# Order of the second expert's loads, of the first dense splits, and the PSUM banks of the dense first layer

## The chip, the core and the metric

One core of one Trainium2 chip runs the whole program. The metric is the device time of one execution in microseconds (us). PE is TensorE, ACT ScalarE, DVE VectorE, POOL GpSimd; SP is the engine whose queue issues nearly all DMAs here.

## What is computed

Three stages follow one another: a gated linear attention, a mixture of eight experts with one expert per token, and a dense layer pair with an ELU between.

```python
# attention, B=4, H=8, S=768, D=48: state over time
state = alpha[t] * state + outer(k[t], v[t]);  y[t] = q[t] @ state
# experts: x [3072, 384], 8 experts, F = 1024
idx = argmax((xn @ en.T) / tau);  gate = softmax(...)[idx]
out[mask] = gate * (relu(x[mask] @ w1[e]) @ w2[e])
# dense: w_in [384, 2048], w_out [2048, 384]
h = x @ w_in;  g = where(h > 0, h, exp(min(h, 0)) - 1);  result = g @ w_out
```

## The kernel before

Every factor of the expert and dense products is split into a high and a low part, and three matmuls (high x high, high x low, low x high) stand for one. ACT makes the high part by a copy with rounding, DVE the low part by a subtraction.

**Attention** (`fast`, `ending`) computes the tokens and scatters each tile of 128 of them with an indirect DMA on POOL (`put`, L583) into the DRAM tensor `xs`, sorted by expert. `load_rows` reads one expert's rows back into the tile `xr`, of which there is one.

**Experts** (`moe1`). A block is (e, f), expert and 128 of its 1024 hidden columns, 64 blocks. `mm1(e, f)` makes `h` in a bank of the pool `psG` (three banks, tag `g`) with 9 matmuls (L996 to L998); ACT makes `hh` (L1000) and DVE `hl` (L1001). `mm2(e, f)`, one block later, adds 9 matmuls to the three banks `y` of the pool `psA` (L1028 to L1030). In blocks f = 4, 5, 6 `turn(e + 1, f - 4)` transposes the next expert's rows from `xr` (L977) and splits them (`evict`, L1018, L1019); after the last of these the next `load_x` goes out. Behind the last block of an expert `y[0]` and `y[2]` are copied by ACT and `y[1]` by DVE (L1038 to L1042) into `x2T`, at a column offset that is known only at run time (`off_i`). Experts are taken in the order of their size; `CAPS` gives the columns each one has, from 432 down to 368. Expert e's columns stand in `x2T` behind those of e - 1.

In the same loop, counted by n, `split_piece` splits the weights of the next expert (L200, L203) and orders the next weight load from SP (L171). `load_d` loads pieces of the dense weights as 64-bit numbers (L224), and `decode` turns them into 32-bit ones: one `Square` on ACT (L242), three operations on DVE (L238 to L240), two on POOL (L243, L244). `split_dense` (L258, L259) splits the decoded weights by blocks of the dense stage: four of `wi` in the last iterations n = 61 to 64, two of `wo`. The iteration n = 64 holds only the last `mm2`.

Between the first two blocks and the rest stands an If (L1055): its usual branch is empty, its Else (`fix`) repairs rare cases and reads and rewrites `xr` and `xs`. Behind the join each engine brings the counts of its semaphores in line (L1055 in the trace).

**Dense** (`moe2`). u counts six groups of 512 columns, m sixteen blocks of 128 of the 2048 hidden columns. `mm1(u, m)` makes `h` from `xh`, `xl` with 9 matmuls (L1184) in a bank of the pool `psH2` (four banks); then follow DVE `mn` = min(h, 0) (L1186), ACT `Exp` (L1187), DVE `g` (L1190), which reads the bank last, ACT `gh` (L1193) and DVE `gl` (L1194), which `flush` issues only in the next block, behind that block's `mn`. `mm2`, three blocks later, makes 12 matmuls into four banks of `psO` (L1205 to L1207). In u = 0 each block also carries two `split_dense`. `load_u(u + 1)` at m = 8 splits the next 512 columns by `split_x` (L1103, L1104). For u = 0 these splits stand in the last `mm2` of the experts, between the copies of `y`.

The order of the instructions of each `manual_schedule` block is written out by hand; instructions of different blocks and the If are put together by the scheduler.

Of the kernel before, what the change touches and what calls it, by code (L numbers as in the profile page):

```python
# [8 lines left out]
F32 = mybir.dt.float32  # L9
F32R = mybir.dt.float32r  # L10
# [9 lines left out]
E, F, F2 = 8, 1024, 2048  # L20
# [10 lines left out]
KD = DM // 128  # L31
# [24 lines left out]
U = 512  # L56
# [6 lines left out]
def fused_kernel(ctx, tc, qk, a, v, emb, w12, wi, wo, cst, sel, cols, out):  # L63
    nc = tc.nc
    PS = bass.MemoryType.PSUM
# [4 lines left out]
    stage = ctx.enter_context(tc.tile_pool(name="stage", bufs=2 * PIECES))  # L70
# [81 lines left out]
    raw, whi, wlo = {}, {}, {}  # L152
# [67 lines left out]
    def load_d(j, pool):  # L220
        if j < len(dq):
            nm, s, src = dq[j]
            t = pool.tile([128, HS], I64, bufs=2, name="raw64")
            nc.sync.dma_start(out=t, in_=src[:, s * HS:(s + 1) * HS])  # L224
            dbuf[j] = t
# [726 lines left out]
    def moe1(x2T, xr0, t0, fix, es):  # L952
        with ExitStack() as st:
            xT_p = st.enter_context(tc.tile_pool(name="xT", bufs=2, side="right"))
            h_p = st.enter_context(tc.tile_pool(name="h", bufs=2, side="right"))
            xr, xT, hb, acc = {0: xr0}, {}, {}, {}
            first, freed = [], []

            def load_x(e):
                if e < E:  # L960
                    xr[e] = xr_p.tile([128, 4, DM], F32, name="xr")
                    load_rows(xr[e], e, [0, DM], puts[-2:-1] if e == 1 else [])

            def turn(e, kk):
                if e >= E:
                    return
                if kk == 0:
                    xT[e] = (xT_p.tile([128, KD, CAP], F32R, tag="xh", name="xh"),
                             xT_p.tile([128, KD, CAP], F32R, tag="xl", name="xl"))
                t = psT.tile([128, CAPR], F32, name="t") if e else t0[kk]  # L970
                blocks = 4 if CAPS[e] > 384 else 3
                for r in range(blocks):
                    pr = min(128, CAPR - r * 128)
                    w = min(128, CAP - r * 128)
                    rows = xr[e][:pr, r, kk * 128:(kk + 1) * 128]
                    if e:
                        nc.tensor.transpose(t[:, r * 128:r * 128 + pr], rows, c["ident"][:pr, :pr])  # L977
                    else:
                        nc.tensor.matmul(t[:, r * 128:r * 128 + w], rows, c["ident"][:pr, :w], start=False, stop=(r == 3))
                evict(e, kk, t)  # L980
                if kk == KD - 1:
                    xr.pop(e)
                    if e:
                        load_x(e + 1)
# [36 lines left out]
            def mm2(e, f):  # L1021
                if f == 0:
                    acc[e] = [psA.tile([128, CAP], F32, name=f"y{d}")[:, :CAPS[e]] for d in range(KD)]
                n = CAPS[e]
                hh, hl = (h[:, :n] for h in hb.pop((e, f)))
                for d in range(KD):
                    wh, wl = wblk(e, f * FW + DM + d * 128, 128)
                    nc.tensor.matmul(acc[e][d], wh, hh, start=(f == 0), stop=False)  # L1028
                    nc.tensor.matmul(acc[e][d], wh, hl, start=False, stop=False)  # L1029
                    nc.tensor.matmul(acc[e][d], wl, hh, start=False, stop=(f == FB - 1))  # L1030
                if f == FB - 1:
                    o1 = nc.scalar.value_load(off_i[0:1, e:e + 1], min_val=0, max_val=N)
                    o2 = nc.vector.value_load(off_i[0:1, e:e + 1], min_val=0, max_val=N)
                    y = acc.pop(e)
                    if e == E - 1:
                        for nm in ("xh2", "xl2"):
                            first.append([stage.tile([128, U], F32R, tag="raw", name=nm) for _ in range(KD)])
                    nc.scalar.activation(out=x2T[:, 0, bass.ds(o1, n)], in_=y[0], func=AF.Copy)  # L1038
                    nc.vector.tensor_copy(x2T[:, 1, bass.ds(o2, n)], y[1])
                    if first:  # L1040
                        split_x(x2T, *first, 0, 0)
                    nc.scalar.activation(out=x2T[:, 2, bass.ds(o1, n)], in_=y[2], func=AF.Copy)  # L1042
                    if first:
                        split_x(x2T, *first, 0, 1)
                        split_x(x2T, *first, 0, 2)

            EARLY = 2
            with tc.manual_schedule():
# [17 lines left out]
            psT = st.enter_context(tc.tile_pool(name="psT", bufs=2, space=PS))  # L1066
            dc = st.enter_context(tc.tile_pool(name="dc", bufs=2))
            with tc.manual_schedule():
                load_d(0, dc)
                load_d(1, dc)  # L1070
                load_x(1)
                LAG = 1
                blocks = [(e, f) for e in range(E) for f in range(FB)]
                for n in range(EARLY, len(blocks) + LAG):
                    if n < len(blocks):
                        e, f = blocks[n]
                        mm1(e, f)
                        if n == EARLY:
                            mm2(*blocks[n - LAG - 1])
                        if f >= 4 and f < 4 + KD:  # L1080
                            turn(e + 1, f - 4)
                    if n >= LAG:
                        mm2(*blocks[n - LAG])
                    if n > 2:
                        split_piece()
                        if n % 2:
                            split_piece()
                    if freed:
                        load_d(freed.pop(), dc)
                    j = (n - 2) * 4 // 7  # L1090
                    if j >= 0 and j != (n - 3) * 4 // 7:
                        decode(j, dc, dense)
                        freed.append(j + 2)
                    if n > len(blocks) - 4:
                        split_dense("wi", n - len(blocks) + 3, dense)
                        if n > len(blocks) - 2:
                            split_dense("wo", n - len(blocks) + 1, dense)
            return first, dense

    def split_x(x2T, xh, xl, u, kk):  # L1100

        src = x2T[:, kk, u * U:(u + 1) * U]
        nc.scalar.activation(out=xh[kk], in_=src, func=AF.Copy)  # L1103
        nc.vector.tensor_tensor(xl[kk], src, xh[kk].bitcast(F32), op=ALU.subtract)  # L1104
# [43 lines left out]
    def moe2(x2T, first, dense):  # L1148
        with ExitStack() as st:
# [2 lines left out]
            g_p = st.enter_context(tc.tile_pool(name="g2", bufs=5))  # L1152
            o_p = st.enter_context(tc.tile_pool(name="o2", bufs=5))
            psO = st.enter_context(tc.tile_pool(name="psO", bufs=4, space=PS))
            psH = st.enter_context(tc.tile_pool(name="psH2", bufs=4, space=PS))
            x2, gb, acc, stores = {0: first}, {}, {}, []
            low = []

# [14 lines left out]
                x2[u] = (xh, xl)  # L1173

            def mm1(u, f):
                ps = psH.tile([128, U], F32, name="h2")
                xh, xl = x2[u]
                wh, wl = dblk("wi", f)
                w = [(wh[:, kk * 128:(kk + 1) * 128], wl[:, kk * 128:(kk + 1) * 128]) for kk in range(KD)]
                terms = [t for kk in range(KD) for t in ((w[kk][0], xh[kk]), (w[kk][1], xh[kk]), (w[kk][0], xl[kk]))]  # L1180
                if u == f == 0:
                    terms = [terms[n] for n in (0, 1, 3, 4, 6, 7, 2, 5, 8)]
                for n, (l, x) in enumerate(terms):
                    nc.tensor.matmul(ps, l, x, start=(n == 0), stop=(n == len(terms) - 1))  # L1184
                mn = e_p.tile([128, U], F32, name="mn")
                nc.vector.tensor_scalar(mn, ps, 0.0, None, op0=ALU.min)  # L1186
                nc.scalar.activation(out=mn, in_=mn, func=AF.Exp)  # L1187
                flush()
                g = e_p.tile([128, U], F32, name="g")
                nc.vector.scalar_tensor_tensor(g, mn, -1.0, ps, op0=ALU.add, op1=ALU.max)  # L1190
                gh = g_p.tile([128, U], F32R, tag="gh", name="gh")
                gl = g_p.tile([128, U], F32R, tag="gl", name="gl")
                nc.scalar.activation(out=gh, in_=g, func=AF.Copy)  # L1193
                low.append(lambda: nc.vector.tensor_tensor(gl, g, gh.bitcast(F32), op=ALU.subtract))  # L1194
                gb[u, f] = (gh, gl)
# [34 lines left out]
            blocks = [(u, m) for u in range(NU) for m in range(M)]  # L1230
# [18 lines left out]

    shared = ExitStack()  # L1250
    psG = shared.enter_context(tc.tile_pool(name="psG", bufs=3, space=PS))
    xr_p = shared.enter_context(tc.tile_pool(name="xr", bufs=1, side="right"))
    x0 = attention()
    with tc.tile_pool(name="x2T", bufs=1) as p, ExitStack() as es:
        x2T = p.tile([128, KD, N + CAP], F32, name="x2T")
        first, dense = moe1(x2T, *x0, es)
        shared.close()
        with tc.manual_schedule():
            moe2(x2T, first, dense)


_OUTS = [((N, DM), "float32")]
# [74 lines left out]
```

## Time and profile before

| | us |
|---|---|
| median of the runs shown (794.42, 795.0, 795.1) | 795.0 |
| the profiled execution, its own time | 796.37 |
| its span, first to last instruction | 794.6 |

| engine | busy us | share of the span |
|---|---|---|
| PE | 768.8 | 97% |
| DVE | 521.5 | 66% |
| ACT | 363.1 | 46% |
| POOL | 188.8 | 24% |

The attention stage ends near 156 us, the experts run to 386 us, the dense stage to the end. The granted TensorE clock is 1.00 in each stretch from 100 us on. In the stretch 200 to 350 us PE is busy for the whole time. The page is read as follows: "busy" is time in instructions, a release in square brackets names what ended the idle time just before an instruction, and a line "x3" merges neighbours of one kind. Matmuls overlap, so their spacing, and not their length, is what one costs.

### The profile page before, as it was taken

To read this page: it belongs to the slowest core of one execution; us is meant where nothing else is said; L and a number is where in the kernel's file an instruction comes from. 1 tells how busy PE (TensorE), PEld (TensorE's weight loads), DVE (VectorE), ACT (ScalarE), POOL (GpSimd) and SP (SyncE) were. 2 spreads that over 40 slices of the span, in tenths; PEclk is the share of its full clock that TensorE was granted. 3 is DMA by queue.
4 is the path that set the end of the run, shared out by engine and by line. 5 is a ranking of instruction groups with operands and counts; after the bars stand their busy time and mean duration, and the time that the engine had idled before them with its cause. 6 is when DMAs were issued, how large, how long until landed. Compare 5 with 4: busy or idle time off the path is not lost.

```text
span 794.6 us, 13699 instructions
## 1 busy us (share of the span) xinstructions
PE 768.8 (97%) x5077; PEld 699.0 (88%) x5077; DVE 521.5 (66%) x1001; ACT 363.1 (46%) x802; POOL 188.8 (24%) x217
## 2 busy tenths in 40 slices
PE   7999998889999999999999999999999999999996
PEld 4888887579999999999898899999999999999996
DVE  6789899946877877896576755454555545545442
ACT  4668787435455455553545433233333323323331
POOL 5544667313433433342000020020002002002002
PEclk9899999999999999999999999999999999999999
DMA  9999873357565666661000010010001001000001
GB/s 240 263 269 246 247 187 96 124 170 195 180 198 186 202 204 202 208 200 44 1 1 1 1 40 1 0 40 1 1 1 40 1 1 40 1 0 33 9 1 40
DMA packets 44804, 77.82 MB, mean 98 GB/s; under 512 B 11958, under 2 KB 18230, under 8 KB 44734
## 3 DMA queue, kind: packets, MB, share of 16 engines
q1 hardware_dynamic: 41662, 67.47, 30.2%
q0 software_dynamic: 3072, 9.45, 3.2%
q8 instruction: 40, 0.66, 0.4%
q14 instruction: 30, 0.25, 0.1%
HBM read 64.69 MB, written 12.22 MB: 97 GB/s over the span
## 4 chain that ended last, share of the span: by engine, by line
PE 38%; issue 30%; DVE 3%; POOL 3%; ACT 2%; DMA 1%; POOLq 0%; SPq 0%; ACTq 0%
PE h L1184 6%; PE y L1028 5%; PE y L1030 4%; PE y L1029 4%; PE h L998 4%; PE h L996 4%; PE h L997 4%; POOL out_dram L1218 2%; PE o L1207 2%; PE o L1205 2%; PE o L1206 2%; PE t L977 1%; DVE dlo L259 1%; DVE g L1190 1%; DVE mn L1186 1%
## 5 line engine op out<-in xcount | busy, mean ns | idle before, releaser
L1186 DVE TENSOR_SCALAR mn<-h 128x512 f32<-128x512 f32 x96 | 66.3, 690 | 139.6 <-PE h L1184 139.6
L1187 ACT ACTIVATE mn<-mn 128x512 f32<-128x512 f32 x96 | 60.7, 632 | 171.7 <-DVE mn L1186 171.7
L1207 PE MATMUL o<-dwo,gl 128*128 128x384 f32 x384 | 129.4, 337 | 1.4 <-DVE gl L1194 1.4
L1206 PE MATMUL o<-dlo,gh 128*128 128x384 f32 x384 | 128.4, 334 | 0.0
L1205 PE MATMUL o<-dwo,gh 128*128 128x384 f32 x384 | 128.2, 334 | 0.0
L1184 PE MATMUL h<-xh,dwi 128*128 128x512 f32 x288 | 112.7, 391 | 0.6 <-ACT x2T L1042 0.6
L1184 PE MATMUL h<-xh,dlo 128*128 128x512 f32 x288 | 113.2, 393 | 0.0
L1184 PE MATMUL h<-xl,dwi 128*128 128x512 f32 x288 | 112.5, 392 | 0.0
L1218 POOL DMA_INDIRECT out_dram<-ob,ids x24 | 23.7, 987 | 340.3 <-ACT ob L1215 336.7
L1193 ACT ACTIVATE gh<-g 128x512 fp32r<-128x512 f32 x96 | 60.7, 633 | 77.9 <-DVE g L1190 77.9
L1000 ACT ACTIVATE hh<-h 128x432 fp32r<-128x432 f32 (+6 forms) x64 | 32.4, 507 | 105.1 <-PE h L998 100.5
L203 DVE TENSOR_TENSOR wlo<-raw,whi 128x512 fp32r<-128x512 f32 x96 | 72.8, 786 | 5.6 <-ACT whi L200 5.6
L1190 DVE SCALAR_TENSOR_TENSOR g<-mn,h 128x512 f32<-128x512 f32 x96 | 66.1, 689 | 15.2 <-ACT mn L1187 14.8
L1205 PEld LDWEIGHTS o<-dwo,gh 128*128 128x128 f32 x384 | 72.0, 187 | 4.2
L1206 PEld LDWEIGHTS o<-dlo,gh 128*128 128x128 f32 x384 | 72.0, 187 | 4.0
L1207 PEld LDWEIGHTS o<-dwo,gl 128*128 128x128 f32 x384 | 72.2, 188 | 2.1 <-DVE gl L1194 1.7
L1028 PE MATMUL y<-hh,whi 128*128 128x432 f32 (+6 forms) x192 | 68.3, 356 | 0.0
L243 POOL TENSOR_SCALAR dg<-dg 128x384 f32<-128x384 f32 x32 | 42.1, 1316 | 107.4 <-ACT dg L242 107.3
L996 PE MATMUL h<-xh,whi 128*128 128x432 f32 (+6 forms) x192 | 66.5, 347 | 0.7 <-ACTq L1055 0.7
L1001 DVE SCALAR_TENSOR_TENSOR hl<-h,hh 128x432 fp32r<-128x432 f32 (+6 forms) x64 | 36.7, 573 | 46.4 <-ACT hh L1000 45.0
L1194 DVE TENSOR_TENSOR gl<-g,gh 128x512 fp32r<-128x512 f32 x96 | 65.7, 684 | 1.2 <-ACT gh L1193 1.1
L998 PE MATMUL h<-xh,wlo 128*128 128x432 f32 (+6 forms) x192 | 66.4, 346 | 0.0
(216 smaller groups left out, 1506.2 us busy)
## 6 DMA issues: line engine op xcount, KB each, us to landing
raw<-in_w_dram SPq DMA_DIRECT2D x96, 256.0 KB, 3.1
qk<-in_qk_dram SPq DMA_DIRECT2D x40, 192.0 KB, 5.0
vt<-in_v_dram SPq DMA_DIRECT2D x24, 256.0 KB, 6.0
raw<-in_wi_dram SPq DMA_DIRECT2D x16, 384.0 KB, 3.8
raw<-in_wo_dram SPq DMA_DIRECT2D x16, 384.0 KB, 3.8
xr<-xs SPq DMA_DIRECT2D x7, 576.0 KB, 5.4
at<-in_alpha_dram SPq DMA_DIRECT2D x40, 99.0 KB, 5.6
xs<-zero SPq DMA_DIRECT2D x7, 288.8 KB, 6.2
```

The source lines that it names most:

```text
L203: nc.vector.tensor_tensor(l[:, sl], r, h[:, sl].bitcast(F32), op=ALU.subtract)
L996: nc.tensor.matmul(ps, wh, xh[:, kk], start=(kk == 0), stop=False)
L998: nc.tensor.matmul(ps, wl, xh[:, kk], start=False, stop=(kk == KD - 1))
L1028: nc.tensor.matmul(acc[e][d], wh, hh, start=(f == 0), stop=False)
L1184: nc.tensor.matmul(ps, l, x, start=(n == 0), stop=(n == len(terms) - 1))
L1186: nc.vector.tensor_scalar(mn, ps, 0.0, None, op0=ALU.min)
L1187: nc.scalar.activation(out=mn, in_=mn, func=AF.Exp)
L1190: nc.vector.scalar_tensor_tensor(g, mn, -1.0, ps, op0=ALU.add, op1=ALU.max)
L1194: low.append(lambda: nc.vector.tensor_tensor(gl, g, gh.bitcast(F32), op=ALU.subtract))
L1205: nc.tensor.matmul(o_, gh[:, sl], wh, start=(f == 0), stop=False)
L1206: nc.tensor.matmul(o_, gh[:, sl], wl, start=False, stop=False)
L1207: nc.tensor.matmul(o_, gl[:, sl], wh, start=False, stop=(f == M - 1))
```

## The change

Four edits. `load_x(1)` is written ahead of the two first `load_d`. The splits of the first 512 dense columns leave the copies of `y` and are written ahead of the last `mm2` of the experts, in iteration n = 64. The dense first layer takes its banks from `psG`, three of them, in place of a pool of four of its own, and its first block uses the usual order of terms. The decodes start at n = 5 and not 2, and end at n = 60 and not 57.

```diff
                     y = acc.pop(e)
-                    if e == E - 1:
-                        for nm in ("xh2", "xl2"):
-                            first.append([stage.tile([128, U], F32R, tag="raw", name=nm) for _ in range(KD)])
                     nc.scalar.activation(out=x2T[:, 0, bass.ds(o1, n)], in_=y[0], func=AF.Copy)
                     nc.vector.tensor_copy(x2T[:, 1, bass.ds(o2, n)], y[1])
-                    if first:
-                        split_x(x2T, *first, 0, 0)
                     nc.scalar.activation(out=x2T[:, 2, bass.ds(o1, n)], in_=y[2], func=AF.Copy)
-                    if first:
-                        split_x(x2T, *first, 0, 1)
-                        split_x(x2T, *first, 0, 2)
...
+                load_x(1)
                 load_d(0, dc)
                 load_d(1, dc)
-                load_x(1)
...
+                    if n == len(blocks):
+                        for nm in ("xh2", "xl2"):
+                            first.append([stage.tile([128, U], F32R, tag="raw", name=nm) for _ in range(KD)])
+                        for kk in range(KD):
+                            split_x(x2T, *first, 0, kk)
                     if n >= LAG:
                         mm2(*blocks[n - LAG])
...
-                    j = (n - 2) * 4 // 7
-                    if j >= 0 and j != (n - 3) * 4 // 7:
+                    j = (n - 5) * 4 // 7
+                    if j >= 0 and j != (n - 6) * 4 // 7:
                         decode(j, dc, dense)
...
-            psH = st.enter_context(tc.tile_pool(name="psH2", bufs=4, space=PS))
...
-                ps = psH.tile([128, U], F32, name="h2")
+                ps = psG.tile([128, U], F32, tag="g", name="h2")
...
-                if u == f == 0:
-                    terms = [terms[n] for n in (0, 1, 3, 4, 6, 7, 2, 5, 8)]
...
-    xr_p = shared.enter_context(tc.tile_pool(name="xr", bufs=1, side="right"))
+    rest = ExitStack()
+    xr_p = rest.enter_context(tc.tile_pool(name="xr", bufs=1, side="right"))
...
-        shared.close()
+        rest.close()
         with tc.manual_schedule():
             moe2(x2T, first, dense)
+        shared.close()
```

## Rows read from the trace of the kernel before

**Rows 1.** Waits of PE: who waited for whom, us in total, times, longest.

```profile
PE o L1207 <- DVE gl L1194: 1.4, 1, 1.4
...
PE t L977 <- DMA xr<-xs: 1.2, 1, 1.2
...
PE h L1184 <- ACT x2T L1042: 0.6, 1, 0.6
```

**Rows 2.** Timeline of SP's queue: start us, length us, instruction.

```profile
166.68 0.82 SPq L224 DMA_DIRECT2D raw<-in_wi_dram  x2
172.58 1.23 SPq L274 DMA_DIRECT2D xr<-xs  x2
...
196.87 4.72 SPq L171 DMA_DIRECT2D raw<-in_w_dram  x3
201.63 0.43 SPq L224 DMA_DIRECT2D raw<-in_wi_dram  x1
```

**Rows 3.** Instructions of line 1055, the If: count, ns each, first and last start.

```profile
L1055 SPq EVENT_SEMAPHORE  x9: 17/17/17, 168.1 to 171.4; - x9
...
L1055 SPq COMPARE_BRANCH  x1: 73/73/73, 167.5 to 167.5; - x1
```

**Rows 4.** Timeline of PE across the transposes of expert 1, two blocks.

```profile
175.18 0.36 PE L998 MATMUL h<-xh,wlo 128*128 128x432 f32 x1
...
177.40 0.46 PE L1028 MATMUL y<-hh,whi 128*128 128x432 f32 x1
...
180.84 0.36 PE L998 MATMUL h<-xh,wlo 128*128 128x432 f32 x1
...
181.66 0.46 PE L1028 MATMUL y<-hh,whi 128*128 128x432 f32 x1
```

**Rows 5.** Timeline of PE from the experts into the dense stage.

```profile
386.12 0.33 PE L1029 MATMUL y<-hl,whi 128*128 128x368 f32 x1
386.29 0.33 PE L1030 MATMUL y<-hh,wlo 128*128 128x368 f32 x1
...
389.59 0.39 PE L1184 MATMUL h<-xh,dwi 128*128 128x512 f32 x1
...
395.83 0.33 PE L1205 MATMUL o<-dwo,gh 128*128 128x384 f32 x1
```

**Rows 6.** Timeline of ACT in the same stretch.

```profile
384.41 0.52 ACT L258 ACTIVATE dwo<-wd 128x384 fp32r<-128x384 f32 x1
...
386.70 0.46 ACT L1042 ACTIVATE x2T<-y 128x368 f32 x1
387.06 1.14 ACT L1103 ACTIVATE xh<-x2T 128x512 fp32r<-128x512 f32 x2
388.10 0.52 ACT L258 ACTIVATE dwi<-wd 128x384 fp32r<-128x384 f32 x1
388.51 0.52 ACT L258 ACTIVATE dwo<-wd 128x384 fp32r<-128x384 f32 x1
```

**Rows 7.** Timeline of DVE in the same stretch.

```profile
385.09 0.55 DVE L259 TENSOR_TENSOR dlo<-wd,dwo 128x384 fp32r<-128x384 f32 x1
...
387.71 1.30 DVE L1104 TENSOR_TENSOR xl<-x2T,xh 128x512 fp32r<-128x512 f32 x2 [0.19 <-ACT xh L1103]
...
389.39 0.55 DVE L259 TENSOR_TENSOR dlo<-wd,dwo 128x384 fp32r<-128x384 f32 x1
389.86 0.68 DVE L1186 TENSOR_SCALAR mn<-h 128x512 f32<-128x512 f32 x1
```

**Rows 8.** Timeline of DVE and PE around the tenth and the thirteenth dense block.

```profile
430.99 0.69 DVE L1190 SCALAR_TENSOR_TENSOR g<-mn,h 128x512 f32<-128x512 f32 x1 [0.16 <-ACT mn L1187]
...
432.73 0.39 PE L1184 MATMUL h<-xh,dwi 128*128 128x512 f32 x1
```

**Rows 9.** Timeline of DVE and PE in expert 1's third block.

```profile
202.67 0.60 DVE L1001 SCALAR_TENSOR_TENSOR hl<-h,hh 128x432 fp32r<-128x432 f32 x1
...
203.91 0.35 PE L1029 MATMUL y<-hl,whi 128*128 128x432 f32 x1
```

## The prediction

> **What bounds the kernel now.** I read three views, in this order. First the waits of PE: behind the branch PE waits for another engine or a DMA only three times, 1.2 us for the second expert's rows, 0.6 us at the start of the dense stage, 1.4 us for one `gl` [rows 1]. So from 177 us on the end of the kernel is PE's own work plus those three waits, and what an edit is worth is what it takes off them. Then PE's timeline around each wait, for its full price, which is more than the idle time since the pipeline fills again. Last the timelines of ACT, DVE and SP's queue, for what ended each wait and what comes late next.
>
> The 1.4 us wait decides how the dense part of the change is to be counted. In the first 512 columns (u = 0) ACT and DVE also split the dense weights, and they work as one chain, each step waiting for the other: `mn`, `Exp`, `g`, `gh`, two `split_dense`, next `mn`. It hangs on the first `mn` at 389.86 [rows 7] and not on PE, which is several us ahead of it. Its period is a little longer than PE's, and at the ninth block, with `load_u(1)` added to it, PE catches up with it and waits 1.4 us for `gl` [rows 1]. The next blocks each start as their `gl` arrives. So time that PE gains before 389 us is given back there, except for what the chain gains too.
>
> **Part 1, the second expert's rows first.** SP's queue now issues the two 64-bit loads at 166.68, then the branch, and behind the branch stand nine semaphore waits from 168.1 to 171.4; only then does `load_x(1)` go out, at 172.58 [rows 2, 3]. The nine waits bring the counts of SP's DMA semaphores in line after the If, so they wait for the two 64-bit loads to land. The loads, later in the program than the branch, were drawn ahead of it by the scheduler. `load_x(1)` can't be: the Else path reads and writes that tile. Inside one hand-ordered block the queue keeps the written order even where a later load would be ready: the 64-bit load at 201.63 goes out behind the three weight loads that began at 196.87 and were waiting for DVE [rows 2]. So with `load_x(1)` at the head of the block, the 64-bit loads must follow it behind the branch, and the nine waits no longer contain them. `load_x(1)` still waits for the last scatters into `xs`, as the 64-bit loads do before 166.68. I put its issue 1.2 us after that (172.58 less 171.4, the cost of the register load and address), at about 167.9. From issue to PE's first transpose it took 4.0 us (172.58 to 176.6, which is 177.40 less the 0.8 us of a turn without a wait, below), so it would come at about 171.9. PE is ready for it at 175.4, after the last matmul of that block at 175.18 [rows 4]. If the 64-bit loads were served ahead of it, with the 4.7 us that they now take (166.68 to 171.4), it would come no earlier than now: that is the lower bound.
>
> What the wait costs: from the last first-layer matmul to the first `y` matmul across a transpose, 175.18 to 177.40 is 2.22 us; the next block without a wait takes 180.84 to 181.66, 0.82 us [rows 4]. Gain **1.40 us**, bounds 0 (that case, or the queue's order doesn't change) and 1.40. Nothing after it gives it back: until 386 us PE has no other wait [rows 1], and DVE follows PE there.
>
> The 64-bit loads come about 2 us later, and the decodes are moved by three blocks, so nothing waits for them. Of the moved step every instruction counts: 4 per decode on DVE and ACT, two on POOL, and on SP the load of the piece after next. DVE had room at the end (it does nothing but `hl` in blocks 59 and 60), and the last decode comes a block before the first `split_dense`, which reads other pieces. The new positions (n - 5 in place of n - 2, both in steps of 4 per 7 blocks) meet every phase of the 8 blocks of an expert once in 56 blocks, as the old ones do; only the expert differs. The tightest place now is expert 1's third block, where `hl` ends at 203.27 and PE takes it at 203.91: 0.64 us [rows 9]. That phase now falls on expert 4. Blocks are shorter there: a `y` matmul of 368 columns is spaced 0.17 us [rows 5], so 36 columns less on 18 matmuls make 0.30 us a block, 0.6 us over the two blocks in which DVE falls behind. The 0.64 us are used up. Cost 0 to 0.3 us, I take **0.05 us**.
>
> **Part 2, the dense start.** Now PE ends `y` with the matmul at 386.29, waits until ACT's copy of `y[2]`, issued from L1042, frees the bank, and reaches block (0, 1) at 389.59 [rows 1, 5]. Without a wait the first dense matmul would start at 386.46, and with 27 matmuls from 389.59 to 395.83 (0.231 each) block (0, 1) at 388.54: PE alone would gain 1.05 us. The `psG` banks are free by then (last read by expert 7's `hl`, ahead of the `dlo` at 385.09 [rows 7]), and the splits are made ahead of `y`. But by the chain, the gain is the shift of the first `mn`. I lay out the new order with the spacings of the rows [rows 6, 7]. ACT: `dwo` at 384.41, 0.41 later the three `xh`, 0.52 apart (1.14 less 0.62 for two), the third ending at 386.49; then `y[0]`. DVE: `dlo` at 385.09, `xl` at 385.56, 386.17 and 386.78 (spacing 0.61), the third ending at 387.47. All stand before PE's terms ask for them: the third, sixth and ninth matmul of 386.46, that is 386.92, 387.62 and 388.31, so the usual order of terms costs nothing (0.6 us to spare). Here is the new wait: the copy of `y[2]` writes at an offset known only at run time into the columns that `xl` reads, so it waits for the third `xl`: 387.50 to 387.96. Behind it on ACT stand `dwi` (387.86) and `dwo` (388.27 to 388.79); on DVE their `dlo` at 388.40 and 388.87, and 0.47 later `mn`, at **389.34** in place of 389.86. PE's block ends before (388.70), so it isn't PE that holds it.
>
> Gain **0.52 us**. Bounds: 1.05 if the copies of `y` don't wait for the splits (then all of PE's gain is kept), and 0 if register loads on ACT or DVE stand in the way. I take the value laid out; it comes from the nearest rows.
>
> **Three banks for four.** `h` of block n + 3 needs the bank of block n, free when `g` of n is done. The tightest row: `g` of block (0, 9) ends at 431.68 and block (0, 12) starts at 432.73, 1.05 us later, with four banks [rows 8]. `gl` of a block is issued behind `mn` of the next one, so close to a whole period of the chain after its `g`, while PE asks for it only 2.4 us after that bank (nine matmuls of 0.231 and two of 0.17); so `gl` stays the wait that ends last. Cost **0**, bounds 0 and 0.5 (my 0.52 us of lost distance still leave 0.5). The Trainium skill speaks against this part: Perfetto Trace Analysis, Optimization Strategy, says that a gap that repeats on the engine that should be saturated can mean too few buffers for the next tile. By it the first blocks of u = 0 would show a gap each; by the row they would not, and the sum stays.
>
> **The sum.** 1.40 + 0.52 - 0.05 = 1.87 us. The profiled execution took 796.37 us (span 794.6), so it would take 794.5. The median of the runs shown is 795.0, 1.4 us below that execution; the same 1.87 us off it give **793.1 us**, 0.24% faster. Less than about 0.2% (1.6 us, so anything above 793.4) can't be told from no change.
>
> **Rivals.** (a) The 64-bit loads are still drawn ahead of the branch, so `load_x(1)` goes out as late as now. For: the scheduler did it once. Against: the kept order at 201.63. Only 0.5 us are left: 794.5. (b) The dense start gives nothing, because the chain starts no earlier: 1.40 - 0.05, 793.6. For: the same instructions stand between the last `hl` and `mn`, in another order only. Against: the layout above. (c) All of PE's 1.05 us is kept, because the copies don't wait: 792.6. (d) Slower: DVE falls behind in the expert stage. Place: the block with the copies of `y`, a split and a decode, and the next with two splits and a decode, now in shorter blocks. It decides once `hl` comes after PE wants it, so when the 0.64 us are gone, and the price is each excess. If all 8 rounds of decodes had 0.6 us too much, 4.8 us: 797.9. Against: only one round has this phase, so one excess and not eight.
>
> **How the numbers follow.** Forecast (both parts as laid out) 0.62; (a) 0.12; (b) 0.09; (c) 0.12; (d) 0.05. The forecast is within about 0.4 us of 793.1, as the runs shown spread by 0.7 us; about three quarters of it lies below 793.4. Faster by over 0.2%: 0.48 from it, 0.12 from (c), 0.03 from (b), 0.63 together. Slower 0.05. The rest, 0.32, is within. The range takes in (c) and most of (a): 792.3 to 794.5.
>
> **What would show it.** Part 1: SP issues the rows of expert 1 near 168 us and the 64-bit loads behind them; PE's wait on `xr` at L977 is gone; PE is 1.4 us earlier at 200 us. Part 2: the first dense matmul follows the last `y` matmul by 0.17 us, `mn` comes about 0.5 us earlier against it, and PE's wait for `gl` grows from 1.4 to about 1.9 us. No wait of PE on `g`. Wrong: `load_x(1)` at 172 us; a wait on `hl`; or the wait for `gl` no longer than now (then all of 1.05 us is kept).

## The result, and the profile after

The changed kernel takes 807.35 us (median of 4 runs, 806.47 to 808.43); the kernel before, run beside it, 794.71 (794.33 to 795.1). The ratio is 1.0147, 95% interval 1.0122 to 1.0173: about 12 us slower, where 1.9 us faster was forecast. The profiled execution took 807.04 us, with a span of 805.3. Line numbers shift with the change: the `o` matmul of L1207 stands at L1201 here, the `idl` transfers of L1225 at L1219.

First the waits of PE in the changed kernel (who waited for whom, us in total, times, longest):

```profile
PE y L1028 <- ACT hh L1000: 8.9, 1, 8.9
...
PE o L1201 <- DVE gl L1188: 1.6, 1, 1.6
...
PE y L1029 <- DVE hl L1001: 0.5, 1, 0.5
```

Against [rows 1], the wait of 1.2 us for `xr` is gone, as forecast, and so is the 0.6 us at the dense start. The wait for `gl` is 1.6 us in place of 1.4. New is a single wait of 8.9 us for `hh`, in the expert stage's last blocks. PE's timeline shows it, and what follows it:

```profile
379.43 0.33 PE L998 MATMUL h<-xh,wlo 128*128 128x368 f32 x1
388.68 0.67 PE L1028 MATMUL y<-hh,whi 128*128 128x368 f32 x1 [8.92 <-ACT hh L1000]
389.88 0.68 PE L1029 MATMUL y<-hl,whi 128*128 128x368 f32 x1 [0.53 <-DVE hl L1001]
390.36 0.51 PE L1030 MATMUL y<-hh,wlo 128*128 128x368 f32 x1
390.66 0.51 PE L1028 MATMUL y<-hh,whi 128*128 128x368 f32 x1
...
397.11 0.33 PE L1030 MATMUL y<-hh,wlo 128*128 128x368 f32 x1
397.28 0.39 PE L1178 MATMUL h<-xh,dwi 128*128 128x512 f32 x1
```

The matmuls behind the wait come 0.30 us apart (390.36 to 390.66), where the same matmul is spaced 0.17 us in [rows 5]. The table by stretches gives the clock that goes with it (us; busy of PE, PEld, DVE, ACT, POOL; granted clock, share of the DMA engines, GB/s):

```profile
350.00:378.00 28.00, 28.00 (x168) 27.93 (x168) 19.99 (x34) 11.99 (x25) 9.55 (x9) 1.00 0.29 82
378.00:389.00 11.00, 2.08 (x12) 1.74 (x10) 1.28 (x3) 1.29 (x4) 0.65 (x1) 0.72 0.53 36
389.00:393.00 4.00, 3.47 (x11) 3.12 (x11) 3.04 (x5) 0.82 (x3) 1.63 (x2) 0.50 0.00 0
393.00:397.00 4.00, 4.00 (x26) 4.00 (x25) 2.03 (x5) 2.54 (x6) 0.00 (x0) 1.00 0.05 0
```

PE stood idle for 8.9 us; the granted clock is 0.50, the 1.2 GHz level, while it starts again, and 1.00 behind 393 us. So the stall costs 11.6 us: 9.1 from 379.60, when the first `y` matmul was due, to 388.68; 0.5 for `hl`; 2.0 for matmuls at the lower clock (from 388.68 to 393.09 pass 4.4 us, where eleven spacings of 0.17 make 1.9; the 2.5 between are these 0.5 and 2.0). All other changes together are worth less than 2 us.

Who holds `hh`? ACT's timeline:

```profile
373.74 0.48 ACT L1000 ACTIVATE hh<-h 128x368 fp32r<-128x368 f32 x1 [2.56 <-PE h L998]
387.71 0.55 ACT L242 ACTIVATE dg<-raw 128x384 f32<-128x384 f32 x1 [13.50 <-DMA raw<-in_wo_dram]
388.16 0.46 ACT L1000 ACTIVATE hh<-h 128x368 fp32r<-128x368 f32 x1
```

ACT stood for 13.5 us at the `Square` of the last decode, in iteration n = 60, because the last 64-bit load had not landed; `hh` of the block that PE had finished was queued behind it. And the load was late because of SP's queue:

```profile
358.19 1.76 SPq L224 DMA_DIRECT2D raw<-in_wo_dram  x2
360.24 15.73 SPq L1219 DMA_DIRECT2D idl<-xs  x3
377.20 0.35 SPq L224 DMA_DIRECT2D raw<-in_wo_dram  x1
```

Between the last but one and the last 64-bit load stand three `idl` transfers, which belong to the dense stage: at its head (L1217 to L1219) it copies the token numbers of each expert's rows from `xs` to `idl`, eight transfers of up to 432 numbers, which nobody needs before the first stores. They write one tensor, so each waits until the one before has landed, and SP waits with it. The load's buffer was free at 366.6 us, behind the last read of decode 29 on DVE:

```profile
366.06 0.56 DVE L240 SCALAR_TENSOR_TENSOR wd<-raw,wd 128x384 int32<-128x384 int32 x1
```

It went out at 377.2 and landed at 387.6 by the trace's DMA events. In the kernel before, the same stretch of SP's queue reads:

```profile
359.13 0.37 SPq L224 DMA_DIRECT2D raw<-in_wo_dram  x1
359.79 52.42 SPq L1225 DMA_DIRECT2D idl<-xs  x7
```

There the last 64-bit load is ahead of all seven; the eighth, which is the first in order, went out at 174.7 us.

At the front of the stage the change did what it should. SP now issues the rows of expert 1 first, in place of [rows 2]:

```profile
167.09 1.22 SPq L274 DMA_DIRECT2D xr<-xs  x2
168.43 0.97 SPq L224 DMA_DIRECT2D raw<-in_wi_dram  x2
```

### The profile page after: what moved, and what is told of

It is laid out like the page before. It is cut to its first block, busy times and chain, and to the rows that moved or that the text cites. A ratio compares the mean times of both kernels' runs of the same rounds, so it can differ in the third digit from the quotient of the medians.

```text
span 805.3 us, 13698 instructions
## 1 busy us (share of the span) xinstructions
PE 769.9 (96%) x5077; PEld 698.9 (87%) x5077; DVE 524.1 (65%) x1001; ACT 362.3 (45%) x802; POOL 188.0 (23%) x217
## 4 chain that ended last, share of the span: by engine, by line
PE 36%; issue 30%; DVE 5%; DMA 3%; POOL 2%; ACT 2%; SPq 0%; POOLq 0%; ACTq 0%
PE h L1178 6%; PE y L1028 4%; PE y L1029 4%; PE y L1030 4%; PE h L997 4%; PE h L998 4%; PE h L996 4%; POOL out_dram L1212 2%; PE o L1201 2%; PE o L1199 2%; PE o L1200 2%; DMA idl<-xs 2%; DVE dlo L259 1%; DMA raw<-in_wo_dram 1%; PE t L977 1%
## 5 line engine op out<-in xcount | busy, mean ns | idle before, releaser
L1201 PE MATMUL o<-dwo,gl 128*128 128x384 f32 x384 | 129.9, 338 | 1.6 <-DVE gl L1188 1.6
L203 DVE TENSOR_TENSOR wlo<-raw,whi 128x512 fp32r<-128x512 f32 x96 | 75.4, 812 | 5.3 <-ACT whi L200 4.5
L1201 PEld LDWEIGHTS o<-dwo,gl 128*128 128x128 f32 x384 | 72.1, 188 | 3.2 <-DVE gl L1188 2.6
L243 POOL TENSOR_SCALAR dg<-dg 128x384 f32<-128x384 f32 x32 | 41.8, 1305 | 127.8 <-ACT dg L242 127.6
L1029 PE MATMUL y<-hl,whi 128*128 128x432 f32 (+6 forms) x192 | 67.0, 349 | 0.5 <-DVE hl L1001 0.5
L1030 PE MATMUL y<-hh,wlo 128*128 128x432 f32 (+6 forms) x192 | 66.9, 348 | 0.0
```

The costliest lines, as they stand in the source:

```text
L203: nc.vector.tensor_tensor(l[:, sl], r, h[:, sl].bitcast(F32), op=ALU.subtract)
L1201: nc.tensor.matmul(o_, gl[:, sl], wh, start=False, stop=(f == M - 1))
```

## The experiments

**How they are read.** The attention stage, which no kernel here changes, ended at other times in each execution: the first `h` matmul of the experts came between 157.5 us and 164.8 us in the 14 profiled ones. That alone spreads the times by several us, and a difference of 1 or 2 us stays inside the intervals of most comparisons. Behind that point, and behind the wait on `xr`, kernels with the same instructions repeat within about 0.05 us, with two exceptions: 0.27 us that ACT loses at one dense block of some kernels (last paragraph), and 0.25 us in e11 at block 53, where a 64-bit load landed 6.3 us after its issue (5.1 in e1) and its decode waited. So beside the measured ratio, each experiment is read by three stretches of its PE timeline, as differences from the kernel before (us, minus is faster). The stretches: from the first `h` matmul of block 3 to that of block 7 (17.72 us before, the wait on `xr` lies in it), from there to the last `y` matmul (198.50), and from that to the last instruction (408.30).

| kernel | block 3 to 7 | block 7 to last y | last y to end | sum |
|---|---|---|---|---|
| after | -1.39 | +11.80 | -0.16 | +10.25 |
| e1_decode_back | -1.39 | 0.00 | -0.45 | -1.84 |
| e2_shift_only | +2.48 | +11.00 | +0.01 | +13.49 |
| e3_idl_in_order | -1.39 | +0.19 | -0.18 | -1.38 |
| e4_idl_ahead | -0.56 | +27.28 | 0.00 | +26.72 |
| e5_dense_only | -1.12 | 0.00 | -0.14 | -1.26 |
| e6_load_only | -1.39 | 0.00 | 0.00 | -1.39 |
| e7_shift_one | -1.40 | 0.00 | -0.42 | -1.82 |
| e8_shift_two | -1.39 | +2.52 | -0.15 | +0.98 |
| e9_last_load_on_act | -1.39 | +0.21 | -0.42 | -1.60 |
| e10_three_banks | -0.95 | +0.01 | +0.01 | -0.93 |
| e11_low_part_on_pool | -1.40 | +0.24 | -1.37 | -2.53 |
| e12_spread_low | -1.40 | 0.00 | -2.23 | -3.63 |

Kernels that keep the old order of the first loads (e2, e4, e5, e10) differ in the first column without a change there: their wait on `xr` hangs on when attention's last scatter lands. That was 6.8 us behind the first `h` matmul in the profile before, with a wait of 1.2 us; 7.8 us in e2 with 2.2 us, 6.2 us in e4 with 0.6, 5.8 us in e10 with 0.2, and 5.7 us in e5 with 0.05. In e2 the lower clock comes on top (0.51 from 175.5 to 179.0 us, behind the wait), so its stretch is longer by 2.48 us and not by 1.0.

The sum for the changed kernel, 10.25 us, is less than the 12.6 us between the medians: the two profiled executions differ by 10.67 us (807.04 and 796.37), and the one of the kernel before took 1.7 us more than its median.

**The decodes put back (e1).** The changed kernel with one part undone.

```diff
-                    j = (n - 5) * 4 // 7
-                    if j >= 0 and j != (n - 6) * 4 // 7:
+                    j = (n - 2) * 4 // 7
+                    if j >= 0 and j != (n - 3) * 4 // 7:
```

> The changed kernel with one part undone: the decodes of the 64-bit weights go back to n - 2; load_x(1) first, the splits ahead of y and the shared banks stay. Theory (the shifted schedule lets three idl transfers stand on SP's queue ahead of the last 64-bit load): the last load goes out ahead of idl e = 1 again, PE's 8.9 us wait on hh is gone, and against the kernel before it gains 1.4 us (wait on xr) plus 0.1 to 0.4 us (first mn 0.42 earlier, of which the changed kernel's chain gave 0.28 back), so 1.5 to 1.8 us, ratio 0.998. Rival R1 (the later decode by itself holds ACT and PE, whatever is on SP's queue): the same, as the decode is early again. Rival R2 (dense start or three banks) and R3 (order of the first loads): still 12 us slower than before.

Measured: 794.12 us beside 793.61, ratio 0.9992 (0.9966 to 1.0017). By the table 1.84 us are gained, at the upper end of the 1.5 to 1.8 expected; the times alone don't tell it from no change. The wait on `hh` is gone, and SP's queue has the load ahead of the transfers again:

```profile
355.29 0.37 SPq L224 DMA_DIRECT2D raw<-in_wo_dram  x1
355.94 47.48 SPq L1219 DMA_DIRECT2D idl<-xs  x7
```

So neither the order of the first loads nor the dense start costs anything. That leaves the shift of the decodes, by SP's queue or by itself.

**The shift alone (e2).** In the kernel before:

```diff
-                    j = (n - 2) * 4 // 7
-                    if j >= 0 and j != (n - 3) * 4 // 7:
+                    j = (n - 5) * 4 // 7
+                    if j >= 0 and j != (n - 6) * 4 // 7:
```

> The kernel before with one part of the change alone: decodes at n - 5. Theory: three idl transfers ahead of the last 64-bit load on SP, a wait of PE on hh of 8 to 10 us near 380 us and a low granted clock after it, 11.5 to 12.5 us slower than before. R1: the same. R2 and R3: no change (within 0.5 us).

Measured: 807.05 us, ratio 1.0150 (1.0105 to 1.0195); PE waits 7.6 us for `hh`, and the stretch with the stall is 11.00 us longer. So the shift brings the stall by itself. It is 0.8 us shorter than in the changed kernel because PE came to block 7 1.2 us later (188.00 against 186.81), while the load landed at the same time (387.55 against 387.63).

```profile
PE y L1028 <- ACT hh L1000: 7.6, 1, 7.6
```

**The transfers kept behind the loads (e3).** Decodes late as in the changed kernel, but the loop over `idl` moves from the head of `moe2` into the expert stage's hand-ordered block, behind its last iteration.

```diff
                             split_dense("wo", n - len(blocks) + 1, dense)
+                for e in range(E):
+                    o3 = nc.sync.value_load(off_i[0:1, e:e + 1], min_val=0, max_val=N)
+                    nc.sync.dma_start(out=idl[bass.ds(o3, CAPS[e])], in_=xs[bass.ds(expert(e) * REG, CAPS[e]), DM:])
             return first, dense
...
-            for e in range(E):
-                o3 = nc.sync.value_load(off_i[0:1, e:e + 1], min_val=0, max_val=N)
-                nc.sync.dma_start(out=idl[bass.ds(o3, CAPS[e])], in_=xs[bass.ds(expert(e) * REG, CAPS[e]), DM:])
```

> The changed kernel, decodes still at n - 5, but the eight idl transfers are written at the end of the expert stage's hand-ordered block, behind the last 64-bit load. Theory: the load goes out when its buffer comes free (near 366 us) and lands in some 3.8 us, 370.5, ahead of ACT's decode at 374; PE's wait on hh is gone; 1.3 to 1.6 us faster than before (1.40 less 0.20 at the hl of expert 4's third block, plus 0.1 to 0.4 of the dense start), ratio 0.998. R1 (the later decode by itself): still 11 to 12 us slower than before. R2, R3: the same 11 to 12 us slower.

Measured: 794.04 us, ratio 0.9998 (0.9973 to 1.0022), by the table 1.38 us faster. SP sends the last three 64-bit loads one behind another, the last at 365.04 us as its buffer comes free, and the transfers behind them (first fence), and ACT's last decode doesn't wait (second):

```profile
356.56 8.81 SPq L224 DMA_DIRECT2D raw<-in_wo_dram  x3
366.18 47.82 SPq L1097 DMA_DIRECT2D idl<-xs  x7
```

```profile
372.46 0.54 ACT L242 ACTIVATE dg<-raw 128x384 f32<-128x384 f32 x1
```

This takes the rival R1 (the later decode costs by itself) away: with the decode just as late and the transfers behind it, the 11 us are gone.

**The transfers put ahead without the change (e4).** The kernel before, decodes early, with four transfers written ahead of the last 64-bit load.

```diff
+                    if n == 54:
+                        for e in range(4):
+                            o3 = nc.sync.value_load(off_i[0:1, e:e + 1], min_val=0, max_val=N)
+                            nc.sync.dma_start(out=idl[bass.ds(o3, CAPS[e])], in_=xs[bass.ds(expert(e) * REG, CAPS[e]), DM:])
                     if freed:
                         load_d(freed.pop(), dc)
...
-            for e in range(E):
+            for e in range(4, E):
```

> The kernel before, decodes at n - 2 and nothing of the change; only the idl transfers of regions 0 to 3 are written ahead of the last 64-bit load (in pass n = 54 of the expert loop). Theory: each idl transfer waits 7.5 us for the one before, so the load goes out some 22 us late and lands 10 us after that; ACT's decode in pass 57 waits 10 to 15 us for it and PE 5 to 10 us, 8 to 13 us slower than before. R1, R2 and R3: no change, since the decodes, the dense start and load_x stand as before.

Measured: 821.35 us, ratio 1.0317 (1.0269 to 1.0366). The mechanism is there without any edit of the change, but larger than I wrote: the load is held for 24.2 us (SP, first two lines) and ACT waits 28.2 us for it (third).

```profile
359.14 24.22 SPq L1091 DMA_DIRECT2D idl<-xs  x4
383.42 0.66 SPq L224 DMA_DIRECT2D raw<-in_wo_dram  x1
```

```profile
394.57 0.55 ACT L242 ACTIVATE dg<-raw 128x384 f32<-128x384 f32 x1 [28.21 <-DMA raw<-in_wo_dram]
```

I had taken three iterations between load and decode for some 20 us; they are 3.1 to 3.5 us each. With so little cover, the 24 us on SP and 11 us of landing (383.42 to 394.48 by the DMA events) leave PE waiting 24.7 us for `hh`.

**One part of the gain at a time (e5, e6).** e5 is e1 with the old order of the first loads, so the dense start alone (first diff). e6 is the kernel before with `load_x(1)` first (second).

```diff
-                load_x(1)
                 load_d(0, dc)
                 load_d(1, dc)
+                load_x(1)
```

```diff
+                load_x(1)
                 load_d(0, dc)
                 load_d(1, dc)
-                load_x(1)
```

> The kernel before with the dense start alone (splits ahead of y, shared banks); the two 64-bit loads again ahead of load_x(1), decodes at n - 2. Theory: up to the last y no step differs from before; the first mn comes 0.42 to 0.44 us earlier after it and keeps that to the end, PE's wait for gl is 1.6 us in place of 1.4; 0.4 us faster, ratio 0.9995. R2 (the dense start or the three banks cost time): a wait of PE on g, or mn no earlier, 0 or slower.

> The kernel before with load_x(1) written ahead of the two 64-bit loads and nothing else. Theory: PE's wait of 1.2 us on xr is gone, PE is 1.4 us earlier from block 7 on and keeps that to the end, ratio 0.998. R3 (the order of the first loads costs time, the 64-bit loads then coming late for the first decode at n = 2): a wait of ACT or DVE on raw64 that reaches PE, so 0 or slower.

Measured: ratios 1.0000 (0.9981 to 1.0018) and 1.0001 (0.9983 to 1.0018), which settle nothing at this size. By the table, e6 gains the 1.39 us of the changed kernel and keeps them. e5 gains only 0.14 us behind the last `y`, not the 0.43 expected: `mn` of the first block comes 0.44 us earlier, but 0.27 us are lost at block (0, 3), as in the changed kernel (below).

**One and two blocks of shift (e7, e8).** The changed kernel with n - 3 or n - 4 in place of n - 5. On SP's queue one `idl` transfer then stands ahead of the last load, or two. The edit of e7, and of e8 with 4 and 5:

```diff
-                    j = (n - 5) * 4 // 7
-                    if j >= 0 and j != (n - 6) * 4 // 7:
+                    j = (n - 3) * 4 // 7
+                    if j >= 0 and j != (n - 4) * 4 // 7:
```

> The changed kernel with the decodes at n - 3 in place of n - 5, so that one idl transfer (e = 1) stands on SP's queue ahead of the last 64-bit load in place of three. Theory: nothing lies ahead of that idl, so the load is not held on SP and only shares the queues with it; PE's wait on hh between 0 and 1 us, so 1.8 to 0.8 us faster than before. R1 (each block of shift costs by itself, a third of 11.6): 2 us slower than before.

> The changed kernel with the decodes at n - 4: two idl transfers ahead of the last 64-bit load. Theory: the load waits for the second idl, so for one landing of 7.5 us, goes out near 370 us and lands near 380, where ACT wants it 3.3 us earlier than in the changed kernel: a wait of PE on hh of 3 to 6 us, 2 to 5 us slower than before. R1 (a third of 11.6 for each block): 6 us slower.

Measured: e7 793.73 us, ratio 0.9983 (0.9961 to 1.0005); e8 799.76, ratio 1.0044 (1.0021 to 1.0067). By the ratio e8 is 1.7 to 5.3 us slower, by the table of its one profile 0.98; its executions spread from 794.5 to 802.25 us, and what makes the difference is not shown. SP and ACT of e7:

```profile
358.52 0.63 SPq L1219 DMA_DIRECT2D idl<-xs  x1
359.71 0.34 SPq L224 DMA_DIRECT2D raw<-in_wo_dram  x1
```

```profile
369.39 0.57 ACT L242 ACTIVATE dg<-raw 128x384 f32<-128x384 f32 x1
```

and of e8:

```profile
361.08 7.84 SPq L1219 DMA_DIRECT2D idl<-xs  x2
369.10 1.61 SPq L224 DMA_DIRECT2D raw<-in_wo_dram  x1
```

```profile
379.05 0.55 ACT L242 ACTIVATE dg<-raw 128x384 f32<-128x384 f32 x1 [5.72 <-DMA raw<-in_wo_dram]
```

With one transfer ahead SP isn't held and nobody waits, though the load lands only just in time (at 369.30 by the trace's DMA events, for the decode at 369.39); with two it is held for the first one's landing and ACT waits 5.7 us, PE 1.1 for `hh` and 0.8 for `hl`, and 2.5 us are lost in the stretch. So the stretch costs 0, 0, 2.5 and 11.8 us for n - 2 to n - 5 (0.09 and 0.19 of the last two are `hl`, below): not a price for each block, as R1 had it, but for each transfer behind the first, less what the blocks in between cover.

**The last load from another queue (e9).** Late decodes, three transfers on SP as in the changed kernel; ACT issues the one load.

```diff
-            nc.sync.dma_start(out=t, in_=src[:, s * HS:(s + 1) * HS])
+            eng = nc.scalar if j == len(dq) - 1 else nc.sync
+            eng.dma_start(out=t, in_=src[:, s * HS:(s + 1) * HS])
```

> The changed kernel, decodes at n - 5 and the idl transfers as there, but the last 64-bit load alone is issued by ACT in place of SP. Theory (SP's queue holds the load, not the transfers as such): it goes out when its buffer comes free, near 366.6 us, while idl transfers are on their way; if it lands in 3.8 us, at 370.4, ACT's decode at 374 doesn't wait; if it lands in 8.6 to 10.4 us as behind them, near 376, ACT waits about 2 us, which PE's distance of 4.6 us to hh covers. Either way PE's wait on hh is gone and the time is 1 to 1.6 us below before (ACT waits up to 2 us for the buffer at the issue, which may cost PE 0 to 0.5). Rival (the idl transfers slow every load, whoever issues it, enough to stop PE): a wait of PE on hh of several us remains.

Measured: 794.60 us, ratio 0.9988 (0.9968 to 1.0008), 1.60 us faster by the table. SP's transfers run at the same time (first fence), ACT's load goes out at 371.40 and its decode (L243 here, as the edit adds a line) doesn't wait:

```profile
364.94 26.19 SPq L1220 DMA_DIRECT2D idl<-xs  x4
```

```profile
371.40 0.38 ACTq L225 DMA_DIRECT2D raw<-in_wo_dram  x1
...
378.80 0.54 ACT L243 ACTIVATE dg<-raw 128x384 f32<-128x384 f32 x1
```

The transfers as such do no harm here. It is their place ahead of the load in one queue.

**Three banks alone (e10).** In the kernel before:

```diff
-            psH = st.enter_context(tc.tile_pool(name="psH2", bufs=4, space=PS))
+            psH = st.enter_context(tc.tile_pool(name="psH2", bufs=3, space=PS))
```

> The kernel before with three banks in place of four for the dense first layer, and nothing else. Prediction's step: no block waits for g, every step after the attention stage as before within 0.05 us. R2 (three banks cost time): waits of PE on g, up to 0.5 us in all.

Measured: one execution of 796.44 us. Behind block 7 every stretch is as before within 0.01 us, and PE nowhere waits for `g`: three banks are free of cost here.

**Two versions to beat both (e11, e12).** In the first 512 columns the chain of ACT and DVE sets the pace, and `load_u(1)` adds 1.8 us to it at m = 8. e11 (e1 besides) gives its three low parts to POOL:

```diff
...
-        nc.vector.tensor_tensor(xl[kk], src, xh[kk].bitcast(F32), op=ALU.subtract)
+        (low_on or nc.vector).tensor_tensor(xl[kk], src, xh[kk].bitcast(F32), op=ALU.subtract)
...
-                    split_x(x2T, xh, xl, u, kk)
+                    split_x(x2T, xh, xl, u, kk, nc.gpsimd if u == 1 else None)
```

e12 (e7 besides) spreads it over three blocks, each `xl` in DVE's idle time between `g` and the first `dlo`:

```diff
...
+                    kk = m - M // 2
+                    if u == 0 and 0 < kk <= KD:
+                        xh, xl = x2[1]
+                        src = x2T[:, kk - 1, U:2 * U]
+                        nc.vector.tensor_tensor(xl[kk - 1], src, xh[kk - 1].bitcast(F32), op=ALU.subtract)
                     if u == 0:
                         split_dense("wi", m + 4, dense)
                         split_dense("wo", m + 2, dense)
-                    if m == M // 2:
+                    if u == 0 and 0 <= kk < KD:
+                        if kk == 0:
...
+                        nc.scalar.activation(out=x2[1][0][kk], in_=x2T[:, kk, U:2 * U], func=AF.Copy)
+                    if u and m == M // 2:
                         load_u(u + 1)
```

> A version to beat both: the changed kernel with the decodes back at n - 2, and the three low parts of load_u(1) (xl, 1.89 us on DVE in the first 512 columns, where the chain of ACT and DVE sets the pace) made by POOL, which is idle there. By the chain: the period of block (0, 8), 6.06 us, falls to 4.25 plus 0 to 0.5 for the three xh on ACT, so 1.3 to 1.8 us more than with the decodes back alone; 3.0 to 3.6 us faster than before in the stages behind attention, and PE's wait for gl shrinks from 1.6 to 0 to 0.4 us. Rival (PE or another engine is next): less than 0.5 us.

> A version to beat both: the changed kernel with the decodes at n - 3 (one idl transfer ahead of the last load), and load_u(1) spread over three blocks: one xh on ACT behind each block's two splits of m = 8, 9, 10, and its xl on DVE in the next block between g and the first dlo, where DVE is idle for 1.17 us each block (an xl takes 0.63). By the chain: the 1.8 us that load_u(1) adds to block (0, 8) are gone, PE's wait of 1.6 us for gl too; 1.40 + 0.43 + 1.6 to 1.8 = 3.4 to 3.6 us faster than before in the stages behind attention, ratio 0.996. Rival (the xl delays dlo and so mn in each of the three blocks, by its 0.63 us or more): 1.8 us of the 3.5, that is no better than with the low part on POOL.

Measured: e11 794.15 us beside 794.98, ratio 0.9976 (0.9952 to 1.0000), by the table 0.92 us more than e1 in the last stretch and not 1.3 to 1.8, and 0.69 in the sum, with the late load at block 53. e12 **792.91 us beside 795.43, ratio 0.9964 (0.9949 to 0.9979)**: faster than the kernel before, the only version here whose interval says so, and than the changed kernel with its ratio of 1.0147; 3.63 us by the table, the 1.80 us of `load_u(1)` gone whole and with it PE's wait for `gl`. DVE in e12, block (0, 10):

```profile
428.21 0.69 DVE L1184 SCALAR_TENSOR_TENSOR g<-mn,h 128x512 f32<-128x512 f32 x1 [0.16 <-ACT mn L1181]
428.82 0.69 DVE L1233 TENSOR_TENSOR xl<-x2T,xh 128x512 fp32r<-128x512 f32 x1
430.07 0.56 DVE L259 TENSOR_TENSOR dlo<-wd,dwi 128x384 fp32r<-128x384 f32 x1 [0.57 <-ACT dwi L258]
```

The `xl` fits, and DVE still waits 0.57 us for `dwi`. What was missing in e11 shows on POOL (first fence) and DVE (second), in that order:

```profile
426.92 4.25 POOL L1101 TENSOR_TENSOR xl<-x2T,xh 128x512 fp32r<-128x512 f32 x3 [6.24 <-ACT xh L1100]
```

```profile
422.16 0.56 DVE L259 TENSOR_TENSOR dlo<-wd,dwo 128x384 fp32r<-128x384 f32 x1
422.63 0.68 DVE L1180 TENSOR_SCALAR mn<-h 128x512 f32<-128x512 f32 x1
423.24 0.68 DVE L1188 TENSOR_TENSOR gl<-g,gh 128x512 fp32r<-128x512 f32 x1
...
427.49 1.28 DVE L1188 TENSOR_TENSOR gl<-g,gh 128x512 fp32r<-128x512 f32 x1
428.69 0.68 DVE L1184 SCALAR_TENSOR_TENSOR g<-mn,h 128x512 f32<-128x512 f32 x1
430.54 1.05 DVE L259 TENSOR_TENSOR dlo<-wd,dwi 128x384 fp32r<-128x384 f32 x1 [1.17 <-ACT dwi L258]
```

While POOL works, `gl` takes 1.28 us in place of 0.68 and `dlo` 1.05 in place of 0.56; `g`, which has one input in PSUM, keeps its 0.68.

## Why the prediction was wrong

**The step that failed** is the one that moved the decodes: "the decodes are moved by three blocks, so nothing waits for them". I listed the decode's load among the moved instructions, "on SP the load of the piece after next", and priced none of its place there. The move takes the load past other work on SP's queue. The last one stood, in the kernel before, 0.29 us ahead of seven `idl` transfers that hold SP for 52 us (359.13, 359.79). I had seen in [rows 2] that a written order holds inside one block, and that the scheduler draws work of later blocks ahead of the If; I did not ask what it would draw in while the expert stage's later loads wait for their buffers. It drew in three transfers (e7 and e8: one more for each block of shift from n - 3 on); by which rule it places them, the runs don't show. Of the rivals none was this one; (d), the slower case, was DVE's own delay.

**Its size.** Held on SP for 10.6 us (366.6 to 377.2), then 10.4 us in landing (3.7 in e3, with no transfer ahead), less the distance that ACT and PE had. The lower clock behind the idle time adds 2.0 us, which no step of the prediction had.

**Part 1 held.** `load_x(1)` went out at 167.09 with the 64-bit loads behind it (forecast 167.9), PE's wait on `xr` is gone, the gain is 1.39 us where 1.40 was laid out, and e6 shows it alone. That the number fits so well is owed to comparing with the very profile it was read from. The 1.2 us that it removes are no constant: in five profiles with the old order the wait was 0.05 to 2.2 us, and the stretch 0.3 to 3.9 us longer than with `load_x(1)` first. What the edit gains on the median is not shown; e6's interval allows 1.4 us either way.

**The `hl` at expert 4's third block held too.** The forecast was 0 to 0.3 us, taken as 0.05; the cost is 0.19 us in the changed kernel and in e3 (PE reaches block 48 at 333.84 where 0.98 us less than before would be 333.65), 0.21 us in e9, 0.09 in e8, where the phase falls on expert 3, and 0 in e1 and e7, where it falls on experts 1 and 2.

**Part 2.** The first dense matmul follows the last `y` by 0.17 us, as forecast (397.11, 397.28). The first `mn` comes 0.42 us earlier against it, where the layout had 0.52: the copy of `y[2]` waited 0.69 us for the third `xl` on ACT, the new wait that was named. Of the 0.42 us, 0.27 are lost again at block (0, 3), a term that the sum lacked. PE's wait for `gl` grew to 1.6 us and not to 1.9: in e1, where nothing is lost at (0, 3), PE catches up with the chain three blocks earlier, and 0.34 us of waiting lie in blocks (0, 8) to (0, 10) (12.78 us in all, 12.44 before).

**Three banks at no cost** held in e10 and, with the dense start, in e1 and e7: no wait on `g`, and 1.04 us from the end of `g` to the matmul that needs its bank in e1's tightest block (0.84 us in the changed kernel, at block (0, 3)). A block's `gl` is what PE waits for, as the layout said.

**The sum without the load.** With the decodes at n - 5 and the load not held, e3 gains 1.38 us and e9 1.60 by the table, where 1.87 were forecast: `hl` took 0.2 us in place of 0.05, and the dense start gave 0.18 and 0.42 in place of 0.52. The 1.84 and 1.82 us of e1 and e7 fall on the forecast partly by luck, since there `hl` costs nothing. What failed by more than a few tenths is the one load.

## What to carry to other kernels

When a step moves, follow each of its DMAs on the queue that issues it and read what stands behind it there, from later stages too: the row behind the last load of the stage was the warning here. A chain of small transfers that wait for one another holds an in-order queue for its whole length; write it behind the last load that anyone waits for, or give it a queue of its own. And where the front of a kernel varies by several us from one execution to the next, compare stretches of the traces, not whole times.

## What the runs showed of the hardware

**A load behind small transfers lands late, too.** 384 KB take 3.7 us from issue to landing in e3 (first line); an `idl` transfer of 1.7 KB in 4-byte pieces takes 7.8 us (second).

```profile
raw<-in_wo_dram SPq DMA_DIRECT2D x16, 384.0 KB, 3.7
idl<-xs SPq DMA_DIRECT2D x2, 1.7 KB, 7.8
```

The same load, issued by SP 0.7 to 2.0 us behind such a transfer, landed 10.4 us (after), 9.6 us (e7) and 9.9 us (e8) after its issue, by the trace's DMA events. From ACT's queue in e9 it landed after 4.4 us (371.40 to 375.81). That doesn't show whether the delay belongs to the queue or to the DMA engines: ACT's load went out 6.5 us behind the transfer under way (364.94), and a weight load of 256 KB that SP itself issued 6.6 us behind an `idl` transfer in e1 (168.35, 174.92) landed after 4.3 us as well. The Trainium skill (DMA: Bandwidth & Descriptors, Queues, rings and completion order) says that SP and ACT each have one ring on each of the same 16 engines, and that an engine consumes a ring's descriptors in their order. The 9.6 to 10.4 us behind a transfer on SP's own queue agree with that order; no run here puts ACT's load as close behind one.

**DVE beside POOL.** In e11 operations of DVE with two inputs in SBUF took 0.5 to 0.6 us longer while POOL subtracted, those with one input in PSUM did not. The Trainium skill (SBUF — State Buffer, Who interferes with whom) has this as a rule: a DVE instruction with two SBUF inputs contends with a POOL instruction that reads SBUF, and the order of issue decides which of them waits. The trace agrees in which operations are hit: `gl` 1.28 us in place of 0.68, `dlo` 1.05 in place of 0.56, `g` unchanged.

**A fixed delay on ACT, not explained.** In the dense stage one `Exp` starts 0.37 us after the end of its `mn` in place of 0.1: at the blocks numbered 3 and 58 in after, e3, e5 and e8, at 29 and 88 in e1, e2, e7, e11 and e12, nowhere in before, e4, e6, e9 and e10. At block 3 it lies in the chain and costs 0.27 us; at 29 it is covered. That it sits at the same blocks in several kernels speaks for the place in ACT's program rather than for chance; the runs don't show what it is.
